# PSUM banks handed out by the planner, f16 hidden states, a float32r output projection and a product moved to GpSimd, in a one-core kernel of a gated recurrence and an FFT convolution

## The chip, the cores and the metric

One Trainium2 chip, one of its cores. The metric is the device time of one execution in microseconds (us). The engines are called as the profile calls them: PE (TensorE, its weight loads apart as PEld), DVE (VectorE), ACT (ScalarE), POOL (GpSimd) and SP (SyncE, which here only issues DMAs).

## The reference

Inputs are `x` and `f_logit`, 4 x 6272 x 256 in float32, a `lower_bound` per channel, a projection of 256 x 768, a filter of 6272 x 256 and an output projection of 256 x 256.

```python
sig = 1.0 / (1.0 + np.exp(-f_logit))
f = lower_bound + (1.0 - lower_bound) * sig
i = 1.0 - f
for t in range(S):                       # S = 6272
    h = f[:, t] * h + i[:, t] * x[:, t]
    y[:, t] = h
proj = y @ w_proj
x1, x2, x3 = proj[..., :D], proj[..., D:2*D], proj[..., 2*D:]     # D = 256
x2_conv = irfft(rfft(x2, axis=1) * rfft(filter, axis=0), axis=1)  # length 6272
out = (x1 * x2_conv * x3) @ w_out
```

## The kernel before

Everything runs on one core, batch after batch. The length 6272 is split as 49 x 128. Per batch there are these phases, each a function:

- `hgrn(b)`: 13 chunks of 512 time steps (the last has 128). `f_logit` and `x` are loaded (L238), ACT makes the sigmoid (L241), POOL multiplies (L243), PE transposes both into channel-major form in PSUM banks 6 and 7 (L252), ACT makes the forget gate `fTs` (L262), and DVE runs the recurrence as a scan (L266) into `hs`, float32r, two buffers. POOL copies `hs` as f16 into the long tile `HA` (L269). PE multiplies `hs` by the weights `W13`, float32r, for x1 and x3 (L277, banks 4 and 5); ACT copies x1 to `x1s` (L285) and DVE multiplies x3 by it into `z`, f16 (L288). Each chunk has two halves of 128 channels, `kh` on the way in and `jb` on the way out.
- `wraps()`: DMAs that copy pieces of `HA` into its middle part (L296), so that `phase_p` reads a cyclic sequence.
- `phase_p(b)`: x2, in 13 groups of four rows (L550), copied by ACT or DVE into `X2`.
- `phase_f1(b)`: first DFT step, 16 units (L565), copied into the middle part of `HA`, called `A`.
- `mini(b)`: the columns of frequency zero, which end in `zm`.
- `units(b)`: 16 units. Second DFT step on PE (L616), product with the transformed filter `Hu` on DVE (L626, two per unit), the zero columns from `zm` on POOL (L619), inverse step on PE (L637), copied to `Th` (which lies on `X2`). `Hu` has two buffers; each unit loads it from the DRAM tile `H[u]` by three DMAs (L609).
- `phase_o(b)`: 13 groups of four rows. Last inverse step on PE (L663), product with `z` on DVE into `PP` as f16 (L672), output projection on PE with the weights split into a high and a low f16 part, `Woh` and `Wol` (L685, four matmuls of 256 columns per row), copied to `osb` (L211) and stored (L696).

`prepare` runs once: the weights, the DFT tables, and the filter's transform, which starts with a rotation by a float32 matmul (L479), goes on with two float32r DFT steps (L496, L512) and stores `H[u]` to DRAM, one DMA per unit.

The order of the instructions is written out by a planner at build time. Each step is given to `op` with a cost per engine, the tiles it reads and the tiles it writes. `emit` is a list scheduler: of the steps whose predecessors have been placed it takes the one that can start earliest by its costs, the longest remaining path breaking ties. The order is then fixed in every engine's queue; the chip waits on semaphores. PSUM's banks are named in the steps, so two steps that use the same bank come in their order of declaration. `hgrn(b+1)` is planned together with `units(b)` and `phase_o(b)`, which keep to banks 0 to 3 except in the last batch. `prepare` and `hgrn(0)` are one call of `emit`; `wraps()` of batch 0 and all that follows are the second.

Of the kernel before, what the change touches and what calls it, by code (L numbers as in the profile page):

```python
# [9 lines left out]
F32 = mybir.dt.float32  # L10
# [11 lines left out]
S = 6272  # L22
# [28 lines left out]
class Plan:  # L51
# [5 lines left out]

    LAT = {"PE": 0.2, "ACT": 0.16, "DVE": 0.14, "POOL": 0.16, "SP": 0.0}
    OWN = {"PE": 0.0, "ACT": 0.1, "DVE": 0.08, "POOL": 0.1, "SP": 0.0}

    def __init__(self):
        self.ops, self.writer, self.readers = [], {}, {}
        self.free = {e: 0.0 for e in self.LAT}
        self.dma = 0.0
        self.table = None

    def op(self, cost, fn, r=(), w=(), kb=0.0, table=None):
# [8 lines left out]
        me = len(self.ops)  # L76
        self.ops.append(dict(cost=cost, fn=fn, preds=preds, kb=kb, table=table, end=None,
                             eng=None, succ=[]))
# [16 lines left out]

    def emit(self):
# [8 lines left out]
        while cand:  # L105
            best = None
            for e, f in self.free.items():
                pick = None
                for i in cand:
                    o = ops[i]  # L110
                    if e in o["cost"]:
                        at = max(f, self.ready(o, e))
                        if o["table"] and self.table and o["table"] != self.table:
                            at += 1.3
                        key = (at, -o["level"], i)
                        if pick is None or key < pick:
                            pick = key
                if pick is not None:
                    o = ops[pick[2]]
                    key = (pick[0] + (o["cost"][e] if len(o["cost"]) > 1 else 0.0) * 0.01,  # L120
                           pick[1], pick[2], e, pick[0])
                    if best is None or key < best:
                        best = key
            i, e, at = best[2:]
# [8 lines left out]
            o["fn"](e)  # L133
# [8 lines left out]
def kernel(  # L142
# [59 lines left out]

    def bank(*k):
        return [("b", i) for i in k]
# [23 lines left out]
    def hgrn(b):  # L228
        z = zt[b % 2]
        for c in range(NCHK):  # L230
# [14 lines left out]
            hk = c % 2  # L245
            for kh in range(2):
                cols = slice(kh * 128, kh * 128 + 128)
                sT, uT = PS[:, 6, 0:n], PS[:, 7, 0:n]

                def turn(e, dst, src, cols=cols, nb=nb):  # L250
                    for j in range(nb):
                        nc.tensor.transpose(dst[:, j * 128:(j + 1) * 128], src[:, j, cols],  # L252
                                            iden[:])
                op({"PE": 0.108 * nb}, lambda e, f=turn, d=sT, s=ft: f(e, d, s),
                   r=[("ft", k)], w=bank(6))
                op({"PE": 0.108 * nb}, lambda e, f=turn, d=uT, s=xt: f(e, d, s),
                   r=[("xt", k)], w=bank(7))
                j = count["f"] % 2
                count["f"] += 1
                fT, h = fTs[:, j, 0:n], hs[:, kh, hk, 0:n]  # L260
                op({"ACT": 0.13 + n / 1200.0}, lambda e, fT=fT, sT=sT, kh=kh:
                   nc.scalar.activation(fT, sT, AF.Identity, scale=nomc[:, kh:kh + 1],  # L262
                                        bias=1.0), r=bank(6), w=[("fT", j)])
                init = 0.0 if c == 0 else hs[:, kh, 1 - hk, CH - 1:CH].bitcast(F32)
                op({"DVE": 0.07 + 2.25 * n / 1000.0}, lambda e, h=h, fT=fT, uT=uT, init=init:
                   nc.vector.tensor_tensor_scan(h, fT, uT, init, op0=AOP.mult, op1=AOP.add),  # L266
                   r=bank(7) + [("fT", j), ("h", kh, 1 - hk)], w=[("h", kh, hk)])
                hn = HA[:, HB[kh] + t0:HB[kh] + t0 + n]
                op({"POOL": 0.1 + n / 1000.0}, lambda e, hn=hn, h=h: nc.gpsimd.tensor_copy(  # L269
                    hn, h.bitcast(F32)), r=[("h", kh, hk)], w=[("hn", kh, c)])  # L270
            for jb in range(2):
                for i in range(2):
                    js = slice(i * 256 + jb * 128, i * 256 + jb * 128 + 128)

                    def mm(e, i=i, js=js, hk=hk, n=n):
                        for kh in range(2):
                            nc.tensor.matmul(PS[:, 4 + i, 0:n], W13[:, kh, js],  # L277
                                             hs[:, kh, hk, 0:n], start=(kh == 0),
                                             stop=(kh == 1))
                    op({"PE": 2 * (0.06 + n / 2400.0)}, mm, r=[("h", 0, hk), ("h", 1, hk)],  # L280
                       w=bank(4 + i))
                j = count["s"] % 2
                count["s"] += 1
                xs = x1s[:, j, 0:n]
                op({"ACT": 0.06 + n / 1200.0}, lambda e, xs=xs, n=n: nc.scalar.activation(  # L285
                    xs, PS[:, 4, 0:n], AF.Copy, scale=ZS), r=bank(4), w=[("x1s", j)])
                op({"DVE": 0.07 + n / 960.0}, lambda e, zz=z[:, jb, t0:t0 + n], xs=xs, n=n:
                   nc.vector.tensor_tensor(zz, PS[:, 5, 0:n], xs, op=AOP.mult),  # L288
                   r=bank(5) + [("x1s", j)], w=[("z", b % 2, jb, c)])
# [12 lines left out]
    def prepare(tmp):  # L302
        dve, pool, act = nc.vector, nc.gpsimd, nc.scalar
        raws = [HA[:, S + 4096 * k:S + 4096 * (k + 1)].bitcast(F32)
                .rearrange("m (r d) -> m r d", d=D) for k in range(3)]
        hws = [HA[:, S + 12288 + 2048 * k:S + 12288 + 2048 * k + 1024]
               .rearrange("p (a n) -> p a n", a=2) for k in range(2)]
# [10 lines left out]
        def oms(e):  # L318
# [6 lines left out]
        wp = raws[0][:, 0:6].rearrange("p a d -> p (a d)").rearrange("p (k j) -> p k j", k=2)  # L325
        wo = raws[1][:, 0:2]
        op({"SP": 0.5}, lambda e: nc.sync.dma_start(
            wp, moe_w_proj.rearrange("(a p) j -> p a j", p=128)), w=E(0, 4096), kb=768)
        op({"SP": 0.5}, lambda e: nc.sync.dma_start(
            wo, moe_w_out.rearrange("(a p) j -> p a j", p=128)), w=E(4096, 8192), kb=256)  # L330
        for kh in range(2):
            small(lambda e, kh=kh: dve.tensor_scalar(
                wp[:, kh, :], in0=wp[:, kh, :], scalar1=omc[:, kh:kh + 1], scalar2=None,
                op0=AOP.mult), 768, r=["om"], w=E(0, 4096))
            for i, j0 in enumerate((0, 512)):
                small(lambda e, kh=kh, i=i, j0=j0: dve.tensor_copy(
                    W13[:, kh, i * 256:(i + 1) * 256], wp[:, kh, j0:j0 + 256]), 256,
                    r=E(0, 4096), w=["W13"])
            for p in range(2):
# [3 lines left out]
                    .rearrange("k (e g) -> k e g", e=2)), 256, r=E(0, 4096), w=["W2"])  # L343
        small(lambda e: dve.tensor_copy(Woh[:], wo[:]), 512, r=E(4096, 8192), w=["Wo"])
        small(lambda e: dve.tensor_tensor(Wol[:], wo[:], Woh[:], op=AOP.subtract), 512,
              r=E(4096, 8192), w=["Wo"])
# [105 lines left out]
        rot = tmp.tile([128, 256], F32, name="rot")  # L452
# [10 lines left out]
        small(gaps, 1920, r=["iden"], w=["f2e"], e="POOL")  # L463
# [297 lines left out]
```

## Time and profile before

| what | value |
|---|---|
| median of 3 runs | 731.81 us (728.07 to 734.73) |
| the profiled execution | 733.49 us |
| its span, first to last instruction | 731.7 us |
| mean granted TensorE clock in the span | 0.899 |
| busy: PE, DVE, ACT, POOL | 617.1, 513.9, 379.6, 203.2 us |
| DMA, mean over the span | 173 GB/s |

The span is what the profiled instructions cover; 1.8 us of the execution's own time lie outside it. A busy time counts an engine as busy from the start of an instruction to its modelled end, so PE's counts matmuls that overlap in its pipeline. "Releaser" is what ended an idle time.

### The profile page before, as it was taken

The numbers are of one execution on the slowest core, as the hardware profiler recorded it, in microseconds if no ns is written. First come the engines' busy times: TensorE is split into PE (matmuls) and PEld (weight loads), VectorE is DVE, ScalarE is ACT, GpSimd is POOL, SyncE is SP. The second block draws the span as 40 slices with busy tenths as digits, with TensorE's granted clock in tenths as the row PEclk, the third lists the DMA queues.
The fourth block names the chain that finished last, engine by engine and source line by source line (L and its number), as shares of the span: only waits on it lengthen the run. The fifth ranks groups of instructions, "written<-read, shape, count | busy, mean of one in ns | idle before, by whom it ended". The sixth has DMA issues, their size and how long they took to land. (4 is left out here: it accounts for less than half of the span.)

```text
span 731.7 us, 13373 instructions
## 1 busy us (share of the span) xinstructions
PE 617.1 (84%) x5262; PEld 471.1 (64%) x5262; DVE 513.9 (70%) x572; ACT 379.6 (52%) x485; POOL 203.2 (28%) x256
## 2 busy tenths in 40 slices
PE   4889993588878999888888999978769999677896
PEld 3767772574546887864556887845448888444585
DVE  8987772389787666697877665898676666967542
ACT  4578882485433555774333556854424547422232
POOL 4335451223323332033223333033324310010000
PEclk9999997699887999999778999999978999955599
DMA  9755646336565757155465766155746732034144
GB/s 308 279 167 162 204 151 232 127 88 204 182 194 175 241 194 268 41 175 175 160 201 181 239 216 239 58 168 181 215 149 227 242 151 82 22 115 131 45 193 160
DMA packets 82161, 126.95 MB, mean 173 GB/s; under 512 B 5454, under 2 KB 56722, under 8 KB 81330
## 3 DMA queue, kind: packets, MB, share of 16 engines
q1 hardware_dynamic: 82098, 126.10, 52.8%
q8 instruction: 41, 0.67, 0.4%
q14 instruction: 22, 0.18, 0.1%
HBM read 84.54 MB, written 28.90 MB: 155 GB/s over the span
## 5 line engine op out<-in xcount | busy, mean ns | idle before, releaser
L626 DVE TENSOR_TENSOR PP<-PS,Hu 98x1008 f16<-98x1008 f32 x128 | 147.8, 1198 | 46.1 <-DMA Hu<-H 37.0
L277 PE MATMUL PS<-hs,W 128*128 128x512 f32 (+1 forms) x416 | 140.5, 432 | 16.3 <-ACT x1s L285 10.9
L243 POOL TENSOR_TENSOR XT<-XT,FL 128x1024 f32<-128x1024 f32 (+1 forms) x52 | 116.7, 2244 | 86.0 <-DMA XT<-in_x_dram 61.2
L209 ACT CAST X<-PS 128x784 f16<-128x784 f32 (+2 forms) x86 | 87.1, 1020 | 86.4 <-PE PS L637 71.7
L269 POOL CAST HA<-hs 128x512 f16<-128x512 f32 (+1 forms) x104 | 61.6, 593 | 245.3 <-DVE hs L266 236.1
L266 DVE TENSOR_TENSOR_SCAN hs<-fTs,hs,PS 128x512 fp32r<-128x512 f32 (+1 forms) x96 | 115.9, 1207 | 10.6 <-PE PS L252 8.9
L672 DVE TENSOR_TENSOR PP<-PS,z 128x1024 f16<-128x1024 f32 (+1 forms) x52 | 61.1, 1184 | 82.7 <-PE PS L663 76.8
L262 ACT ACTIVATE fTs<-PS,nomc 128x512 f32<-128x512 f32 (+1 forms) x104 | 69.1, 665 | 80.1 <-DVE hs L266 42.6
L637 PEld LDWEIGHTS <-PP 98*128 98x128 f16 x1024 | 64.3, 118 | 51.0 <-issue 34.2
L685 PE MATMUL PS<-Woh,PP 128*128 128x256 f16 x392 | 90.3, 278 | 3.4 <-DVE PP L672 3.0
L685 PEld LDWEIGHTS <-PP 128*128 128x128 f16 x784 | 82.6, 114 | 15.8 <-issue 7.6
L277 PEld LDWEIGHTS PS<-hs,W 128*128 128x128 f32 x416 | 66.8, 196 | 35.3 <-ACT x1s L285 15.4
L685 PE MATMUL PS<-Wol,PP 128*128 128x256 f16 x392 | 89.0, 275 | 0.0
L616 PE MATMUL PS<-HA,FT 64*128 64x512 f16 x256 | 59.5, 458 | 31.7 <-DVE PP L626 30.3
L637 PE MATMUL PS<-VA,PP 98*128 98x98 f16 x512 | 72.9, 244 | 15.2 <-DVE PP L626 11.7
L211 ACT ACTIVATE osb<-PS 128x1024 f32<-128x1024 f32 (+1 forms) x51 | 50.3, 986 | 66.3 <-PE PS L685 37.5
L241 ACT ACTIVATE FL<-FL 128x1024 f32<-128x1024 f32 (+1 forms) x52 | 52.4, 1008 | 61.5 <-DMA FL<-in_f_logit_dram 61.5
L288 DVE TENSOR_TENSOR z<-PS,x1s 128x512 f16<-128x512 f32 (+1 forms) x104 | 67.1, 645 | 15.6 <-PE PS L277 9.9
L252 PE MATMUL PS<-iden,FL 128*128 128x128 f32 x392 | 67.1, 295 | 12.8 <-ACT FL L241 10.8
L285 ACT ACTIVATE x1s<-PS 128x512 f32<-128x512 f32 (+1 forms) x104 | 59.3, 570 | 28.9 <-DVE z L288 15.8
L637 PE MATMUL PS<-VB,PP 98*128 98x98 f16 x512 | 73.5, 245 | 0.0
L252 PE MATMUL PS<-iden,XT 128*128 128x128 f32 x392 | 69.9, 304 | 3.4 <-DVE hs L266 3.4
(89 smaller groups left out, 711.3 us busy)
## 6 DMA issues: line engine op xcount, KB each, us to landing
FL<-in_f_logit_dram SPq DMA_DIRECT2D x48, 512.0 KB
XT<-in_x_dram SPq DMA_DIRECT2D x48, 512.0 KB
out_dram<-osb SPq DMA_DIRECT2D x48, 512.0 KB
Hu<-H SPq DMA_DIRECT2D x64, 196.0 KB
Hu<-H SPq DMA_DIRECT2D x128, 98.0 KB
HA<-in_moe_filter_fft_dram SPq DMA_DIRECT2D x6, 1024.0 KB
HA<-HA SPq DMA_DIRECT2D x16, 384.0 KB
H<-HA SPq DMA_DIRECT2D x16, 196.0 KB
```

What stands on the lines that cost most here:

```text
L209: nc.scalar.copy(dst, src)
L243: op({"POOL": 0.1 + 0.535 * nb}, lambda e, xt=xt, ft=ft: nc.gpsimd.tensor_tensor(xt, xt, ft, op=AOP.mult), r=[("ft", k)], w=[("xt", k)])
L252: nc.tensor.transpose(dst[:, j * 128:(j + 1) * 128], src[:, j, cols], iden[:])
L262: nc.scalar.activation(fT, sT, AF.Identity, scale=nomc[:, kh:kh + 1], bias=1.0), r=bank(6), w=[("fT", j)])
L266: nc.vector.tensor_tensor_scan(h, fT, uT, init, op0=AOP.mult, op1=AOP.add),
L269: op({"POOL": 0.1 + n / 1000.0}, lambda e, hn=hn, h=h: nc.gpsimd.tensor_copy(hn, h.bitcast(F32)), r=[("h", kh, hk)], w=[("hn", kh, c)])
L277: nc.tensor.matmul(PS[:, 4 + i, 0:n], W13[:, kh, js], hs[:, kh, hk, 0:n], start=(kh == 0), stop=(kh == 1))
L288: nc.vector.tensor_tensor(zz, PS[:, 5, 0:n], xs, op=AOP.mult),
L626: nc.vector.tensor_tensor(PP[:TB, k, o, :, :, 1:64], px.unsqueeze(1).broadcast_to([TB, 2, UE, 63]), hh[:, :, :, 1:64], op=AOP.mult)
L637: nc.tensor.matmul(PS[:, ib + o, pr * TB:(pr + 1) * TB], PP[:TB, k, o, n, 2 * pr:2 * pr + 2, :], v[:TB], start=(n == 0), stop=(n == 1))
L672: nc.vector.tensor_tensor(y, PS[:, cb:cb + 2, 0:rn * 128].rearrange("p a (m i) -> p a m i", i=rn), zr[:, :, :, r0:r0 + rn], op=AOP.mult),
L685: nc.tensor.matmul(po[:, i, :], y[:, kh, :, i], w[:, kh, :], start=(n == 0), stop=(n == 3))
```

## The change

- **Planner.** PSUM has no fixed banks any more. A step that produces in PSUM takes one or two banks (`take`), the steps that read it name it as their source (`src`), and the banks come free when the last of them has been placed. `room` picks the free banks that are free earliest by plan; `held` keeps a step from taking banks while another predecessor of its readers is not placed. Among steps that can start within 0.6 us (`SLACK`) of the earliest, an engine takes the one with the longest remaining path.
- **Hidden states.** The scan writes f16 straight into `HA` and takes its start from the f16 column before; `hs` and POOL's copy (L269) go. `W13` is f16, so x1 and x3 are f16 matmuls.
- **x1*x3.** For one of the two halves (`jb` = 0) ACT copies x3 too, into a single buffer `x3s`, and POOL multiplies; for the other half DVE multiplies as before.
- **Output projection.** `Woh` and `Wol` become one float32r `Wo`; DVE writes the product into a float32r tile `ys` of its own with two buffers, and each row has two matmuls.
- **Filter.** `H[u]` in DRAM holds both arrangements (three DMAs store it, in `prepare`), one DMA per unit loads it, into three buffers. In `prepare` the raw filter comes in 13 loads into six buffers, each is copied to float32r by ACT, DVE or POOL, and the rotation is a float32r matmul.
- **Order.** `wraps()` of batch 0 is planned with `prepare` and `hgrn(0)`. In the middle part of `HA` (16384 columns) the transformed filter waits for its store at columns 6144 to 10240 (before: 12288 to 16384); `wraps` writes columns 0 to 6096 and 10240 to 16384.
- **Memory.** The second buffer of `osb` lies on the end of `X2`, so `phase_p(b+1)` waits for the stores from it, and POOL clears the gaps there again before each `phase_f1`.

The diff, cut (the planner's bookkeeping, the renaming of bank arguments in `phase_p`, `phase_f1`, `mini` and the copies are left out):

```diff
+    SLACK = 0.6
...
+    def room(self, n):
+        best = None
+        for b in range(0, 8, n):
+            if None not in self.bank[b:b + n]:
+                key = (max(self.bank[b:b + n]), n == 1 and self.bank[b ^ 1] is not None, b)
+                if best is None or key < best:
+                    best = key
+        return best
+
+    def held(self, i):
+        return any(self.ops[p]["end"] is None and p != i
+                   for j in self.ops[i]["users"] for p in self.ops[j]["preds"])
...
+                    if o["take"]:
+                        if rooms[o["take"]] is None or self.held(i):
+                            continue
+                        at = max(at, rooms[o["take"]][0])
...
+                    first = min(can)[0] + self.SLACK
+                    pick = min((c for c in can if c[0] <= first), key=lambda c: c[1:])
...
-    W13 = konst.tile([128, 2, 512], F32R, name="W13")
+    W13 = konst.tile([128, 2, 512], F16, name="W13")
-    Woh = konst.tile([128, 2, 256], F16, name="Woh")
-    Wol = konst.tile([128, 2, 256], F16, name="Wol")
+    Wo = konst.tile([128, 2, 256], F32R, name="Wo")
-    hs = konst.tile([128, 2, 2, CH], F32R, name="hs")
+    x3s = konst.tile([128, CH], F32, name="x3s")
-    H = [dram.tile([TB, 2, UE * 64], F16, name=f"H{u}") for u in range(NU)]
+    H = [dram.tile([TB, 2, 2, UE * 64], F16, name=f"H{u}") for u in range(NU)]
...
-                init = 0.0 if c == 0 else hs[:, kh, 1 - hk, CH - 1:CH].bitcast(F32)
+                init = 0.0 if c == 0 else HA[:, t1 - 1:t1]
...
-                op({"POOL": 0.1 + n / 1000.0}, lambda e, hn=hn, h=h: nc.gpsimd.tensor_copy(
-                    hn, h.bitcast(F32)), r=[("h", kh, hk)], w=[("hn", kh, c)])
...
+                if jb:
+                    op({"DVE": 0.07 + n / 960.0}, lambda e, p, zz=zz, xs=xs, n=n:
+                       nc.vector.tensor_tensor(zz, PS[:, p, 0:n], xs, op=AOP.mult),
+                       r=[("x1s", j)], w=[("z", b % 2, jb, c)], src=x13[1])
+                else:
+                    x3 = x3s[:, 0:n]
+                    op({"ACT": 0.06 + n / 1200.0}, lambda e, p, x3=x3, n=n:
+                       nc.scalar.copy(x3, PS[:, p, 0:n]), w=["x3s"], src=x13[1])
+                    op({"POOL": 0.1 + 2.15 * n / 1000}, lambda e, zz=zz, xs=xs, x3=x3:
+                       nc.gpsimd.tensor_tensor(zz, x3, xs, op=AOP.mult),
+                       r=[("x1s", j), "x3s"], w=[("z", b % 2, jb, c)])
...
-        rot = tmp.tile([128, 256], F32, name="rot")
+        rot = tmp.tile([128, 256], F32R, name="rot")
...
+            op({"POOL": 0.1 + 0.3 * rn, "ACT": 0.1 + 0.22 * rn, "DVE": 0.1 + 0.27 * rn},
+               lambda e, raw=raw, fr=fr, rn=rn: copy(e, fr[:, 0:rn], raw[:, 0:rn]),
+               r=et, w=[("af", g % 2)])
...
+            for i, (p0, p1, q0) in enumerate(((0, TB, 0), (0, Q, Q), (Q, TB, 0))):
+                op({"SP": 0.5}, lambda e, hw=hw, u=u, p0=p0, p1=p1, q0=q0, ab=min(i, 1):
+                   nc.sync.dma_start(H[u][p0:p1, ab], hw[q0:q0 + p1 - p0]),
+                   r=ht, w=[("H", u, i)], kb=2 * (p1 - p0))
...
+            h = (b * NU + u) % 3
+            op({"SP": 0.5}, lambda e, h=h, u=u: nc.sync.dma_start(Hu[:TB, h], H[u][:]),
+               r=[("H", u, i) for i in range(3)], w=[("Hu", h)], kb=400)
...
-                    for kh in range(2):
-                        for w in (Woh, Wol):
-                            nc.tensor.matmul(po[:, i, :], y[:, kh, :, i], w[:, kh, :],
-                                             start=(n == 0), stop=(n == 3))
-                            n += 1
-            op({"PE": 0.44 * rn}, proj, ...)
+                    for kh in range(2):
+                        nc.tensor.matmul(po[:, i, :], y[:, kh, :, i], Wo[:, kh, :],
+                                         start=(kh == 0), stop=(kh == 1))
+            po = op({"PE": 0.34 * rn}, proj, r=[("y", yk)], take=2)
...
             hgrn(0)
+            wraps()
             plan.emit()
...
+        ys = cv.tile([128, 2, 2, 512], F32R, name="ys")
+        osb = [cv.tile([128, 4, 256], F32, name="osb0"),
+               X2[:, NEP * TB:NEP * TB + 2048].bitcast(F32).rearrange("p (r e) -> p r e", e=256)]
```

More of the change, by code (lines that the diff above doesn't have):

```diff
@@ L123, in emit @@
                         best = key
+            assert best is not None
             i, e, at = best[2:]
@@ L132, in emit @@
                 o["end"] = self.dma + 1.0
-            o["fn"](e)
+            if o["take"]:
+                o["at"] = b = rooms[o["take"]][2]
+                self.bank[b:b + o["take"]] = [None] * o["take"]
+                o["fn"](e, b)
+            elif o["src"] is not None:
+                q = ops[o["src"]]
+                o["fn"](e, q["at"])
+                q["uses"] = q.get("uses", 0) + 1
+                q["done"] = max(q.get("done", 0.0), o["end"] + self.LAT[e])
+                if q["uses"] == len(q["users"]):
+                    self.bank[q["at"]:q["at"] + q["take"]] = [q["done"]] * q["take"]
+            else:
+                o["fn"](e)
             cand.remove(i)
@@ L282, in hgrn @@
+                    x13.append(op({"PE": 2 * n / 2400.0}, mm,
+                                  r=[("hn", 0, c), ("hn", 1, c), "W13"], w=["qX"], take=1))
                 j = count["s"] % 2
                 count["s"] += 1
[L284 to L289, printed above, removed]
+                xs, zz = x1s[:, j, 0:n], z[:, jb, t0:t0 + n]
@@ L594, in prod @@
                                     op=AOP.add)
-        op({"DVE": 2.0}, prod, r=bank(2, 3) + ["Hm", ("Hm", 0), ("Hm", 1)],
-           w=[("osb", k), "zm"])
+        op({"DVE": 2.0}, prod, r=["Hm", ("Hm", 0), ("Hm", 1)], w=[("osb", 0), "zm"], src=mm)
     def units(b):
@@ L629, in prod, with inv @@
                         op=AOP.mult)
-                op({"DVE": 1.15}, prod, r=bank(xb + o) + [("Hu", k, i) for i in range(3)],
-                   w=[("P", k, o)])
-            def inv(e, k=k, ib=ib):
+                op({"DVE": 1.2}, prod, r=[("Hu", h)], w=[("P", k, o)], src=f2)
+            def inv(e, ib, k=k):
                 for o in range(2):
```

267 lines of the change are left out of this document (128 added, 139 removed).

## The prediction

> **What bounds the kernel now.** I read the page's head first, then cut the span into its phases, then asked who waits in each.
>
> ```profile
> span 731.7 us, 13373 instructions
> PE 617.1 (84%) x5262; PEld 471.1 (64%) x5262; DVE 513.9 (70%) x572; ACT 379.6 (52%) x485; POOL 203.2 (28%) x256
> ```
>
> No engine fills the span, so the bound must change with the phase. The view of busy time by windows, with edges at the phases' first and last instructions (columns: window, length, busy time and instructions of PE, PEld, DVE, ACT and POOL, granted clock, DMA share, GB/s):
>
> ```profile
> 0.00:117.00 117.00, 99.90 (x595) 77.07 (x596) 91.53 (x163) 83.73 (x118) 52.78 (x74) 1.00 0.63 205
> 117.00:135.50 18.50, 0.81 (x4) 0.29 (x3) 0.29 (x1) 2.19 (x3) 4.65 (x4) 0.57 0.92 315
> 160.00:233.00 73.00, 58.06 (x473) 36.61 (x470) 61.42 (x61) 33.25 (x47) 24.98 (x33) 0.88 0.59 184
> 233.00:292.50 59.50, 59.09 (x532) 48.30 (x531) 37.74 (x41) 31.22 (x43) 20.32 (x20) 0.98 0.69 231
> 292.50:320.00 27.50, 24.02 (x258) 22.07 (x257) 19.50 (x16) 21.93 (x22) 4.27 (x4) 0.94 0.21 71
> 320.00:394.00 74.00, 61.02 (x464) 39.30 (x464) 60.24 (x60) 31.09 (x44) 23.67 (x33) 0.81 0.58 181
> 394.00:452.00 58.00, 57.60 (x522) 47.18 (x518) 36.59 (x40) 30.74 (x42) 20.01 (x20) 0.98 0.70 234
> 480.00:551.00 71.00, 54.20 (x444) 35.13 (x443) 56.86 (x57) 29.77 (x42) 21.98 (x31) 0.87 0.60 180
> 551.00:607.00 56.00, 55.86 (x508) 45.58 (x507) 36.56 (x38) 28.12 (x39) 17.36 (x18) 0.98 0.60 206
> 635.00:687.00 52.00, 37.92 (x316) 21.56 (x312) 37.64 (x35) 12.61 (x16) 5.05 (x16) 0.57 0.36 109
> 687.00:731.70 44.70, 36.73 (x392) 32.72 (x392) 15.37 (x14) 12.67 (x13) 0.00 (x0) 0.92 0.37 145
> ```
>
> In order: `prepare` with `hgrn(0)`; a hole; then, three times, `units(b)` with the first half of `hgrn(b+1)` (73, 74 and 71 us; I call it U) and `phase_o(b)` with the second half (59.5, 58 and 56 us; O), each followed by the 27.5 us of `phase_p` and `phase_f1`; last, U and O of batch 3 without a neighbour. O is PE's: busy 59.09 of 59.50, DVE 37.74. U is DVE's as far as it is anyone's: 61.42 of 73, and the rest of DVE's time is waiting. In the hole nothing computes. Who ended those waits (views of the waits: whole span, then 635:688):
>
> ```profile
> DVE PP L626 <- DMA Hu<-H: 37.0, 26, 3.3
> PE PS L550 <- DMA HA<-HA: 17.7, 2, 13.6
> POOL XT L243 <- DMA XT<-in_x_dram: 61.2, 29, 13.2
> DVE PP L626 <- DMA Hu<-H: 9.9, 10, 2.5
> ```
>
> (Total us, number, longest.) The hole is PE waiting for the wraps. DVE's largest wait in U is the filter load: 37.0 us in all, 9.9 of them in the last U, so about 9 in each of the others.
>
> **The change part by part.** Durations, by group of one form, and how closely matmuls follow each other (timeline: start, length; the last three are pieces of the chain that ended last):
>
> ```profile
> L626 DVE TENSOR_TENSOR PP<-PS,Hu 98x1008 f16<-98x1008 f32 x128 | 147.8, 1198 | 46.1 <-DMA Hu<-H 37.0 <-PE PS L616 7.0 <-PE PS L637 2.0
> L277 PE MATMUL PS<-hs,W 128*128 128x512 f32 x384 | 134.4, 443 | 14.6 <-ACT x1s L285 10.9 <-ACT HA L209 2.8 <-DVE z L288 0.9
> L685 PE MATMUL PS<-Woh,PP 128*128 128x256 f16 x392 | 90.3, 278 | 3.4 <-DVE PP L672 3.0
> L685 PEld LDWEIGHTS <-PP 128*128 128x128 f16 x784 | 82.6, 114 | 15.8 <-issue 7.6 <-DVE PP L672 7.2
> L277 PEld LDWEIGHTS PS<-hs,W 128*128 128x128 f32 x416 | 66.8, 196 | 35.3 <-ACT x1s L285 15.4 <-issue 6.6 <-DVE z L288 4.5
> L288 DVE TENSOR_TENSOR z<-PS,x1s 128x512 f16<-128x512 f32 x96 | 64.8, 675 | 11.4 <-PE PS L277 6.4 <-ACT x1s L285 4.9
> L269 POOL CAST HA<-hs 128x512 f16<-128x512 f32 x96 | 59.3, 618 | 226.3 <-DVE hs L266 217.0 <-PE PS L565 9.2
> L285 ACT ACTIVATE x1s<-PS 128x512 f32<-128x512 f32 x96 | 57.1, 595 | 25.4 <-DVE z L288 15.8 <-PE PS L277 4.7 <-DVE PP L672 3.4
> L243 POOL TENSOR_TENSOR XT<-XT,FL 128x1024 f32<-128x1024 f32 x48 | 113.8, 2371 | 84.4 <-DMA XT<-in_x_dram 60.3 <-PE PS L252 12.3 <-ACT x1s L285 3.7
> L479 PE MATMUL PS<-HA,rot 128*128 128x256 f32 x98 | 23.1, 383 | 0.0
> L496 PE MATMUL PS<-D1r,f 128*128 128x128 f32 x128 | 17.1, 277 | 0.0
> 25.88 3.62 PE L479 MATMUL PS<-HA,rot 128*128 128x256 f32 x16
> 105.09 1.09 PE L496 MATMUL PS<-D1r,f 128*128 128x128 f32 x8
> 111.27 1.21 PE L277 MATMUL PS<-hs,W 128*128 128x512 f32 x4
> 293.79 12.21 PE L550 MATMUL PS<-W,HA 128*128 128x256 f16 x95 [0.75 <-issue]
> 288.69 0.47 SPq L296 DMA_DIRECT2D HA<-HA  x1
> 700.84 3.68 PE PS L685 x32
> 704.53 1.00 PE PS L663 x16
> 705.55 1.24 DVE PP L672
> ```
>
> *Projection (PE, in O).* A dense run gives the pace of a matmul: its length less one duration, over the count less one. For f16 of 256 columns (3.68 - 0.278)/31 = 0.110 us, so today's 784 take 86 us, 21.6 per batch. Afterwards 392, f32r, each with a weight load of its own. No row shows f32r at 256 columns. Lower bound: the load hides, 0.110. Upper: it doesn't; L496, f32r of 128 columns, runs at (1.09 - 0.277)/7 = 0.116, so a load costs up to about 0.11 and a matmul 0.22. L277 lies between: (1.21 - 0.443)/3 = 0.256 for 512 columns, where f16 takes twice 0.110 = 0.22. I take the middle, 0.165: 98 x 0.165 = 16.2 per batch, **-5.4** in each O (bounds -10.8 and 0).
>
> [...]
>
> *x1 and x3 in f16.* 0.256 becomes 0.22: 104 per batch x 0.036 = **-3.7** (bounds: 0 where something else ends the matmul, -9 if every second one now waits for a whole load); the two windows of L288 alone (DVE busy and count) show how `hgrn(1)` is shared out:
>
> ```profile
> 160.00:233.00 73.00, 6.79 (x10) 0.88 0.59 184
> 233.00:292.50 59.50, 9.64 (x15) 0.98 0.69 231
> ```
>
> 15 of 26 halves run in O, so -2 there, the rest in U, where PE doesn't bind.
>
> O in all: -7.5. DVE, at 37.74 of 59.5, is not late next, so this is kept; I count **-8** with the freer banks, bounds -3 and -13. Three times: -24.
>
> *Products moved (DVE).* 13 per batch of 0.675 go, 8.8 us; 5 of the 10 in U, 3.4 us. ACT gets 13 copies of about 0.595 (L285), 7.7 us beside its 31 to 33 busy of 73. POOL loses the copy of 0.618 twice per chunk, 15.4 us per batch, and gains one product; L243 at half size is 1.19 us, so 15.4 again: POOL stays where it is. The copy's going also shortens the way from the last scan to the wrap by about 1 us.
>
> *Hu.* With two buffers a load may start when DVE leaves unit u-2 and must land within one unit's 2 x 1.198 = 2.4 us. With three it has 4.8, and SP issues one DMA for three. Longest wait now 3.3, so nearly all of it goes: -2/3 of 9 in each U (PE is late next: 58 us busy of 73, though it overlaps itself there), -8.5 of 9.9 in the last. Bytes stay the same. U: -3.4 - 6 = **-9**, bounds -3 and -14; three times -27. Last U: 16 x 2.4 = 38.4 plus 4 to fill and drain = 43, **-9**.
>
> *Last O.* The chain repeats 3.68 + 1.00 + 1.24 and a little, 6.0 us for two groups. 16 x 0.165 = 2.64 for 3.68: -1 each, 6.5 times: **-6** (bounds -2 and -11).
>
> *Wraps.* In the hole PE resumes 18.5 us after the last scan's stage; in batch 1 the wrap issued at 288.69 lets L550 go on at 293.79, 5.1 us later. So **-13** (bounds -8, if `prepare`'s stores crowd the queue: with 48 DMAs instead of 16 on SP beside the wraps, and -15).
>
> *Prepare.* L479: 98 at (3.62 - 0.383)/15 = 0.216 are 21 us; 49 at 0.165 are 8: PE -13, with f16 x1/x3 -17. Against it 13 copies to f32r, about 1.1 us each by two of L269 or L285, on three engines, and ACT's 7.7 for x3 while ACT has 83.73 of 117 busy. PE is at 99.90; half is kept: **-8** (bounds 0 and -18).
>
> *Costs.* `phase_p(b+1)` may not write `X2` before the last store from `osb`'s second buffer has landed; by the wrap's 5.1 us from issue to use and PE's lead of four groups, +2 or so each, less the 1 us of the copy: **+2** in all (bounds 0 and +12). The gap clearing on POOL hides under the 12.21 us of `phase_p`. DVE's f32r product and the scan's f16 end read PSUM as before: 0.
>
> Sum: -8 - 13 - 27 - 24 - 9 - 6 + 2 = -85. The profiled execution was 733.5, 1.7 over the median; 731.8 - 85 = 647, and I say **648**.
>
> **Rivals.**
> 1. *f32r loads don't hide* (0.22): +5.4 per O and +5 at the end, +21: 669. For: L496. Against: L277, longer than its load.
> 2. *PE goes cold in U.* Granted clock is 0.81 to 0.88 there and 0.57 in the last U, where PE has only the units' work. Less PE work could pull U towards 0.57. PE's 58 busy at 0.88 would be 58 x 0.88/0.57 = 90 at worst, against the 64 I expect; since a slower PE is also a busier one, I price it half way, +13 in each of three U's: 687. [...]
> 3. *The planner's banks miss the chip's timing.* Banks are promised by planned times; where DMA is late, PE stands at the head of its queue for a bank whose reader waits, with everything behind it. Then only engine work goes: U -3, O -5, the rest half (-17): 648 + 85 - 41 = 692.
> 4. *Slower: x3s.* One buffer. ACT's next x3 copy waits for POOL's product, which stands in POOL's queue behind L243, which waits for the load of x (61.2 us in 29 waits, 2.1 mean). ACT then holds everything behind it. At 2.1 us a chunk, 52 x 2.1 = 109: 648 + 109 = 757. It decides once L243's wait, 2.37 and 1.19 together pass a chunk's 9 to 10 us (117/13, 132/13); the mean of 5.7 doesn't, the longest wait of 13.2 does.
> 5. *No net change*: 3 and part of 4 together, 731.
>
> **How the numbers follow.** Forecast (620 to 665) 0.52; rival 1, 0.13; rival 2, 0.10; rival 3, 0.10; better than 620, 0.04; rival 4, 0.06; rival 5, 0.05. The bounds' sum is -119 at best, so 613; to 705 the first four cases are in, and 0.15 is left out. The measurement can't tell less than about 1%, 724 to 739. Faster 0.89, same 0.05, slower 0.06.
>
> **What would show it.** Projection: 392 matmuls, their pace 0.165 in a dense run. Hole: under 6 us between the last scan and `phase_p(0)`. U near 63 us with hardly a wait of DVE for Hu; last U 43 with 2.4 per unit; O near 51, PE still full. Wrong if ACT waits for POOL (rival 4), if waits for PE's banks lead in U (3), or if the clock in U is under 0.75 (2).

## The result, and the profile after

| | before | after |
|---|---|---|
| median | 729.94 us (725.30 to 734.73, 4 runs) | 707.48 us (703.32 to 709.47, 4 runs) |
| profiled execution, its span | 733.49, 731.7 us | 703.32, 701.4 us |

The ratio is 0.9684, 95% interval 0.9604 to 0.9765: 3.2% faster, where 11% were forecast. Of the 85 us, 30 came between the two profiled executions and 22 between the medians. Of four executions below, two of e3_slack0_hilo_dve (660.67 and 662.33 us, for 648.66 and 649.09) and one of e5_no_x (712.24, for 695.67 to 702.49) were slower than the rest, and the time given is the median of the others. First the head of the page of after:

```profile
span 701.4 us, 12441 instructions
PE 584.2 (83%) x4821; PEld 443.0 (63%) x4821; DVE 484.3 (69%) x518; ACT 409.4 (58%) x548; POOL 208.9 (30%) x211
```

The work did shrink: PE lost 33 us, DVE 30, and ACT gained 30. Then the busy time by windows of after (same columns as before). The first five are cut at the first matmul of each `phase_p`; the others are U and O of batch 0, U and O of batch 1, and U and O of the last batch:

```profile
0.00:139.80 139.80, 100.95 (x546) 69.48 (x546) 82.57 (x152) 94.15 (x136) 53.60 (x61) 0.86 0.61 204
139.80:289.50 149.70, 127.22 (x1110) 99.22 (x1109) 105.54 (x94) 87.33 (x111) 45.41 (x40) 0.91 0.69 225
289.50:441.60 152.10, 130.68 (x1129) 100.63 (x1128) 109.95 (x102) 86.40 (x117) 46.27 (x43) 0.91 0.56 184
441.60:588.40 146.80, 130.01 (x1140) 99.59 (x1140) 110.91 (x102) 87.18 (x119) 47.99 (x43) 0.93 0.58 191
588.40:701.40 113.00, 95.30 (x901) 74.05 (x899) 75.37 (x70) 54.28 (x68) 15.64 (x25) 0.92 0.29 104
...
165.30:208.40 43.10, 31.55 (x324) 19.50 (x324) 38.49 (x37) 17.54 (x21) 11.84 (x19) 0.76 0.54 163
208.40:289.50 81.10, 73.60 (x550) 60.39 (x551) 50.12 (x47) 49.50 (x72) 31.72 (x19) 0.98 0.80 269
314.50:365.00 50.50, 36.52 (x344) 21.91 (x342) 40.36 (x39) 19.10 (x27) 12.95 (x21) 0.77 0.50 152
365.00:431.50 66.50, 63.39 (x502) 53.79 (x501) 44.54 (x41) 38.17 (x55) 25.17 (x14) 0.99 0.76 259
611.50:653.50 42.00, 35.13 (x345) 19.54 (x345) 40.36 (x41) 18.23 (x28) 10.07 (x20) 0.88 0.39 126
653.50:701.40 47.90, 38.77 (x320) 35.45 (x317) 17.23 (x17) 15.01 (x19) 1.72 (x2) 0.92 0.34 135
```

Two things stand out. The first part is not 21 us shorter, it is 4 us longer than the 135.5 of before. And U and O are no longer what they were: U of batch 0 has shrunk to 43.1 us and O has grown to 81.1, because nearly all of `hgrn(b+1)` has moved from beside the units to behind them. DVE's scans alone (L305: busy time and count, clock, DMA share, GB/s), in U and in O of batch 0:

```profile
165.30:208.40 43.10, 0.08 (x1) 0.76 0.54 163
208.40:289.50 81.10, 31.11 (x26) 0.98 0.80 269
```

Put against the forecast, with the times from one `phase_p` to the next (P(0) to P(3) are their first matmuls; only for P(0) of before it is the first matmul after the hole, since three come ahead of the hole or in it, at 116.94 and 121.49; the last column is an experiment told below):

| part | before | after | change | forecast | after, with SLACK = 0 |
|---|---|---|---|---|---|
| start to P(0) | 135.5 | 139.8 | +4.3 | -21 | 119.7 (-15.8) |
| P(0) to P(3) | 474.9 | 448.6 | -26.3 | -49 | 432.6 (-42.3) |
| P(3) to the end | 121.3 | 113.0 | -8.3 | -15 | 110.8 (-10.5) |
| span | 731.7 | 701.4 | -30.3 | -85 | 663.1 (-68.6) |

The groups of one form of after, the waits that answer to those of before, and pieces of the timeline and of the chain that ended last:

```profile
L719 PE MATMUL PS<-Wo,ys 128*128 128x256 f32 x392 | 102.3, 406 | 6.8 <-DVE ys L709 6.8
L719 PEld LDWEIGHTS PS<-Wo,ys 128*128 128x128 f32 x392 | 94.1, 325 | 11.4 <-issue 6.8 <-DVE ys L709 3.3 <-ACT osb L249 0.8
L316 PE MATMUL PS<-HA,W 128*128 128x512 f16 x384 | 104.1, 397 | 2.9 <-DVE HA L305 1.4 <-ACT x1s L324 0.9 <-ACT x3s L333 0.6
L528 PE MATMUL PS<-afs,rot 128*128 128x256 f32 x49 | 11.1, 355 | 8.7 <-ACT afs L247 3.3 <-DVE f L252 2.1 <-ACT f L247 1.8
DVE PP L667 <- DMA Hu<-H: 4.8, 3, 2.0
ACT x1s L324 <- POOL z L335: 5.4, 9, 0.9
58.49 2.32 PE L316 MATMUL PS<-HA,W 128*128 128x512 f16 x10
661.32 3.94 PE PS L719 x16
```

The wait for `Hu` has gone from 37.0 to 4.8 us. ACT waits 5.4 us in all for POOL's product. The projection (L719) is the surprise of this view: 16 matmuls, two groups of rows, take 3.94 us in the chain, where 32 took 3.68.

### The profile page after: what moved, and what is told of

It reads as the page before. It is cut to its first block, busy times and chain, and to the rows that moved or that the text cites. A ratio compares the mean times of both kernels' runs of the same rounds, so it can differ in the third digit from the quotient of the medians.

```text
span 701.4 us, 12441 instructions
## 1 busy us (share of the span) xinstructions
PE 584.2 (83%) x4821; PEld 443.0 (63%) x4821; DVE 484.3 (69%) x518; ACT 409.4 (58%) x548; POOL 208.9 (30%) x211
## 5 line engine op out<-in xcount | busy, mean ns | idle before, releaser
L305 DVE TENSOR_TENSOR_SCAN HA<-fTs,HA,PS 128x512 f16<-128x512 f32 (+1 forms) x96 | 115.4, 1209 | 62.6 <-PE PS L288 55.3
L247 ACT CAST X<-PS 128x784 f16<-128x784 f32 (+2 forms) x91 | 90.7, 1010 | 89.7 <-PE PS L677 81.3
L316 PE MATMUL PS<-HA,W 128*128 128x512 f16 (+1 forms) x416 | 106.5, 384 | 4.1 <-DVE HA L305 1.4
L719 PE MATMUL PS<-Wo,ys 128*128 128x256 f32 x392 | 102.3, 406 | 6.8 <-DVE ys L709 6.8
L719 PEld LDWEIGHTS PS<-Wo,ys 128*128 128x128 f32 x392 | 94.1, 325 | 11.4 <-issue 6.8
L335 POOL TENSOR_TENSOR z<-x3s,x1s 128x512 f16<-128x512 f32 (+1 forms) x52 | 63.1, 1213 | 123.1 <-ACT x3s L333 123.0
L709 DVE TENSOR_TENSOR ys<-PS,z 128x1024 fp32r<-128x1024 f32 (+1 forms) x52 | 60.0, 1177 | 44.6 <-PE PS L702 36.7
L288 PEld LDWEIGHTS PS<-iden,XT 128*128 128x128 f32 x392 | 47.1, 147 | 34.3 <-POOL XT L281 21.4
L288 PEld LDWEIGHTS PS<-iden,FL 128*128 128x128 f32 x392 | 47.6, 148 | 28.5 <-ACT FL L279 19.2
L657 PE MATMUL PS<-HA,FT 64*128 64x512 f16 x256 | 47.5, 459 | 20.8 <-ACT X L247 20.1
L316 PEld LDWEIGHTS <-W 128*128 128x128 f16 x416 | 38.8, 101 | 39.0 <-issue 13.4
L702 PE MATMUL PS<-ID,X 64*128 64x128 f16 x784 | 50.9, 314 | 0.7 <-ACT fTs L300 0.3
```

The source lines that it names most:

```text
L247: nc.scalar.copy(dst, src)
L288: nc.tensor.transpose(PS[:, p, j * 128:(j + 1) * 128], src[:, j, cols], iden[:])
L305: nc.vector.tensor_tensor_scan(h, fT, PS[:, p, 0:n], init, op0=AOP.mult, op1=AOP.add),
L316: nc.tensor.matmul(PS[:, p, 0:n], W13[:, kh, js], HA[:, HB[kh] + t0:HB[kh] + t0 + n], start=(kh == 0), stop=(kh == 1))
L335: nc.gpsimd.tensor_tensor(zz, x3, xs, op=AOP.mult),
L709: nc.vector.tensor_tensor(y, PS[:, cb:cb + 2, 0:rn * 128].rearrange("p a (m i) -> p a m i", i=rn), zr[:, :, :, r0:r0 + rn], op=AOP.mult),
```

## The experiments

All are edits of the kernel after. Times are medians, ratios are against the kernel before on the same chip.

**The choice by longest path.** What moved the steps about? The planner's new rule takes, among the steps that can start within 0.6 us, the one with the longest remaining path; the other theory is that the banks do it.

```diff
-    SLACK = 0.6
+    SLACK = 0.0
```

> The changed kernel with SLACK 0.0 for 0.6: an engine takes the step that can start earliest again, banks still handed out by the planner. Theory A (the 0.6 us choice by longest remaining path puts hgrn(b+1) behind units(b), and the filter's DFT behind hgrn(0)): scans come back into U, U 43-52 -> about 60, O with its rest 80-82 -> about 55, phase_p(0) starts near 120 instead of 139.8; about 670 us. Theory B (the handing out of banks does it: the units' pairs of banks are taken ahead and hgrn's single banks find no room): order and time as the changed kernel, 700 to 710. Theory C (only the f32r projection's bare weight loads cost the forecast gain): no change either, 700 to 710.

663.48 us, ratio 0.9006 (0.8923 to 0.9089). With the banks named in the steps as in the kernel before, and 0.6 kept (`take=1` becomes `take=1, only=(6,)` for the first transpose, and so on):

> The changed kernel with each PSUM producer tied to the banks it had before (sT 6, uT 7, x1 4, x3 5, pairs as in the old code), SLACK 0.6 kept. Theory A: the choice still starves hgrn, 700 to 710. Theory B: two to three scans stand again between the units' products, U about 60, O about 55, 670 us; where only U and O are helped and not prepare, 685.

708.36 us, 0.9647 (0.9588 to 0.9705). P(0) comes at 136.1 us there, so the start is late without the free banks too. P(0) to P(3) takes 432.0 us, 16.6 less than in after, and P(3) to the end 137.4, against 113.0 with free banks.

With both undone, the old banks and SLACK = 0, about 665 us were expected. It took 711.24 us, 0.9705 (0.9631 to 0.9780), with P(0) at 133.2, 436.3 to P(3) and 140.9 to the end. (The output of this kernel is not the reference's, and why is open; only its times are used here.) So it takes both: SLACK = 0 gives its 44 us with free banks and nothing with the old ones, and the free banks give 48 us with SLACK = 0 and nothing with 0.6. Neither theory says that.

Where the 20 us of the first part went is seen in the two traces. Busy time by windows of the filter's first DFT step alone (L542: PE, PEld, clock, DMA share, GB/s), first after, then SLACK = 0:

```profile
0.00:50.00 50.00, 2.87 (x16) 2.73 (x16) 0.88 0.83 288
50.00:95.00 45.00, 0.21 (x1) 0.02 (x1) 0.94 0.60 197
95.00:139.80 44.80, 20.26 (x112) 18.17 (x112) 0.74 0.38 119
```

```profile
0.00:50.00 50.00, 2.12 (x16) 1.94 (x16) 0.90 0.82 291
50.00:95.00 45.00, 14.46 (x104) 12.76 (x104) 0.92 0.64 206
95.00:119.70 24.70, 1.11 (x8) 0.97 (x8) 1.00 0.71 249
```

And DVE's scans (L305) in the same windows, after and SLACK = 0:

```profile
50.00:95.00 45.00, 19.09 (x15) 0.94 0.60 197
95.00:139.80 44.80, 2.22 (x3) 0.74 0.38 119
```

```profile
50.00:95.00 45.00, 10.21 (x8) 0.92 0.64 206
95.00:119.70 24.70, 10.91 (x10) 1.00 0.71 249
```

With 0.6 the scans of `hgrn(0)` are taken first (the rule prefers the longer remaining path; that theirs is the longer is inferred), and 112 of 128 matmuls of the filter's DFT come when hardly a scan is left. That DFT is a chain from PE to ACT or DVE and back, so nothing lies beside it: in 95 to 139.8 PE runs at a clock of 0.74. With 0 the two lie beside each other. The wraps' hole has gone in both; in after the filter stands in its place.

**Which of the two plans.** SLACK = 0 in the first call of `emit` only (`prepare`, `hgrn(0)`, wraps), and its mirror, 0 in the second only:

```diff
+            plan.SLACK = 0.0    # e3_slack0_prepare: then 0.6 after emit
             plan.emit()
+            plan.SLACK = 0.0    # e4_late0: 0.6 before it
```

> SLACK 0.0 only while prepare, hgrn(0) and wraps(0) are planned, 0.6 for all that follows. Theory A by place: phase_p(0) starts near 120 as with SLACK 0.0 throughout, the later batches stay at 147 to 152 us from phase_p to phase_p: 707 - 20 = 687. If the whole 44 us hang on the first plan (the order of batch 0 carried on): 665. If on the later plan: 705.

> SLACK 0.6 in the first plan, 0.0 in the second: the mirror of the run with 0.0 in the first alone (666). Theory D (the first plan costs its 20 us by the 0.6 us choice; the rest of the difference in the batches is a draw among orders of about equal worth, in which the changed kernel had a bad one): phase_p(0) at 140, the three batches 416 to 437 together, as in all other variants, and not 449: 680 to 700. Theory A in full (the 0.6 us choice costs in the batches too, by rule): three batches near 425 here. Theory E (order carried on from the first plan): batches stay at 449, 705.

666.20 us, 0.913 (0.9083 to 0.9177), and 689.43 us, 0.9459 (0.9387 to 0.9532). So, with free banks, the first plan alone gives back nearly all of the 44 us that SLACK = 0 gives. (The mirror's 18 are hardly more than the draw between orders that is measured below. Its three batches took 441.2 us, which none of the three theories had.) The first matmul of `phase_p(0)`, timeline of after, of e1_slack0, of e3_slack0_prepare and of e4_late0:

```profile
139.78 1.07 PE L598 MATMUL PS<-W,HA 128*128 128x256 f16 x4
```

```profile
119.71 0.52 PE L598 MATMUL PS<-W,HA 128*128 128x256 f16 x3 [0.26 <-ACT x1s L324]
```

```profile
120.89 0.52 PE L598 MATMUL PS<-W,HA 128*128 128x256 f16 x3 [0.26 <-ACT x1s L324]
```

```profile
136.49 1.07 PE L598 MATMUL PS<-W,HA 128*128 128x256 f16 x4
```

Over all runs told of here with free banks and the wraps in the first plan, P(0) lies at 113.9 to 124.4 us with 0 there and at 139 to 145 with 0.6 (136.5 in e4_late0). The time from P(0) to P(1) tends to follow it: 138 to 145 us with 0, 142 to 156 with 0.6, though the costs and the rule of the second plan may be the same. Why is open. From after to e3_slack0_prepare it falls by 9 us, from 149.7 to 140.9; about 5 of them lie in U of batch 0 (43.1 us at a clock of 0.76 in after, 37.9 at 0.86 in e3_slack0_prepare).

Does it matter that the wraps moved into the first plan? SLACK = 0, and `wraps()` of batch 0 back in the second plan:

> SLACK 0.0 with wraps() of batch 0 planned after the first plan's end again, behind the clearing of X2. Forecast: the hole comes back, phase_p(0) 13 us later: 663 + 13 = 676. If the hole only went because the filter's DFT now runs to the end of the first plan: 663 to 666.

662.95 us, 0.9091 (0.9021 to 0.9161). The hole is back: three matmuls of `phase_p(0)` come at 128.8, and the long run behind the hole starts at 134.95, as in before (135.54), where with SLACK = 0 alone it starts at 121.11.

```profile
134.95 13.34 PE L598 MATMUL PS<-W,HA 128*128 128x256 f16 x95 [5.35 <-DMA HA<-HA]
```

So moving the wraps is worth 14 us where the hole lies, close to the forecast's 13. P(3) comes at 551.7 all the same, for 552.3: the batches behind the hole took 14 us less, and the total showed none of it. Neither reason in the expectation fits.

**The projection.** The two f16 parts back in place of float32r, the planner told 0.44 per row:

```diff
-    Wo = konst.tile([128, 2, 256], F32R, name="Wo")
+    Woh = konst.tile([128, 2, 256], F16, name="Woh")
+    Wol = konst.tile([128, 2, 256], F16, name="Wol")
...
-            po = op({"PE": 0.34 * rn}, proj, r=[("y", yk)], take=2)
+            po = op({"PE": 0.44 * rn}, proj, r=[("y", yk)], take=2)
```

> The changed kernel with the old projection: ys in f16, Woh and Wol, four f16 matmuls per row instead of two f32r. By the paces read from the two traces (392 x 0.234 = 92 us against 784 x 0.109 = 86) PE loses 6 us in all, all of it in O, which PE bounds. Theory C: the projection is what ate the gain, over 20 us faster, 685. Theories A and B: 6 us faster at most, 700.

686.46 us, 0.9352 (0.9298 to 0.9407). With SLACK = 0:

> SLACK 0.0 and the old f16 projection (Woh and Wol) together, everything else of the change kept. If the two losses are separate they add: 663 less the 20 that the old projection gave with SLACK 0.6 = 643. If the projection's 20 us came only from an O overfull with hgrn (SLACK's doing), it gives the 6 us of the paces here: 657.

652.17 us, 0.8905 (0.8821 to 0.8988). Better by 21 and by 11 us. But the planner's cost had changed too, so that was done alone, float32r kept and 0.34 set to 0.47, near what the chip takes (two matmuls of 0.236):

> The changed kernel with SLACK 0.6 and the f32r projection, but the planner is told 0.47 us per row for it (two matmuls at the measured 0.234) instead of 0.34. If the projection cost 20 us because the planner believed it cheap and put the steps behind it at the wrong times, 687 to 692. If it is the matmuls' own pace and their bare loads, 702 to 708.

> SLACK 0.0 and the honest 0.47 us per row for the f32r projection. Each alone gave 44 and 17. If the wrong cost does harm apart from SLACK: 663 - 12 = 651, level with the old projection under SLACK 0.0 (652). If it only misled the 0.6 us choice: 660 to 665.

690.90 us, 0.9456 (0.9390 to 0.9522), and 653.28 us, 0.8956 (0.8889 to 0.9023). Nothing that runs had changed but its order, and 17 and 10 us went. So the totals don't show that the f16 parts are faster.

Is it float32r that makes the matmul slow? The trace of after answers that. The rotation (L528) is float32r of 256 columns too, each matmul with a load of its own, and runs at nearly the f16 pace, 0.13 us for the 0.110 of before (first line; the clock was 1.00). Its loads are shorter than the projection's (next two lines: min/median/max in ns). They read 128 neighbouring elements of `rot`, while the projection's loads read every fourth element of `ys`, except in the last group of a batch, which has one row and so reads neighbours (last line):

```profile
31.88 1.22 PE L528 MATMUL PS<-afs,rot 128*128 128x256 f32 x8 [0.64 <-DVE f L252]
L528 PEld LDWEIGHTS PS<-afs,rot x49: 186/189/333, 15.6 to 46.2; 128*128 128x128 f32 x49
L719 PEld LDWEIGHTS PS<-Wo,ys x392: 186/329/334, 214.8 to 696.1; 128*128 128x128 f32 x196
L719 PEld LDWEIGHTS PS<-Wo,ys x2: 190/191/192, 267.8 to 268.0; 128*128 128x128 f32 x2
```

L528's pace is (1.22 - 0.282)/7 = 0.13 us, with 0.282 as the median duration of these eight. The last line is the same instruction at a step of one, 190 ns for 329, so here it is the step at which `ys` is read that makes the load long. (The f16 loads of before read `PP` at the same step and took 114 ns.) An estimate: 392 matmuls at 0.13 would be 51 us of PE for 92. A `ys` laid out for that was not run.

**Hu.** With SLACK = 0 and only two of the three buffers of `Hu` in use, 689 us were expected if the third buffer cures DVE's waits, 663 to 668 if not. It took 667.81 us, 0.9133 (0.9070 to 0.9196). DVE waits 26.6 us in all for `Hu` there, against 9.2 with three buffers and SLACK = 0. So the third buffer does what the forecast says of it, and the total hardly shows it. (This output is not the reference's either, and why is open.)

**Products.** Both halves multiplied by DVE, no copy of x3, SLACK = 0 (`if jb:` becomes `if True:`), and the same with the f16 parts:

> SLACK 0.0 and both halves of x1*x3 multiplied on DVE from PSUM as before, no copy of x3, nothing on POOL. Forecast's theory: DVE gets 8.8 us per batch back, 3.4 of them in U: 663 + 10 = 673. Rival (the copy on ACT and the queue of POOL cost more than they free): 650 to 660.

> SLACK 0.0, old f16 projection, both halves of x1*x3 on DVE: what is left is the handed-out banks, f16 h, H in three buffers, the f32r rotation and the early wraps. If the two losses add: 663 - 11 - 9 = 643. If both only loosened the same O: 650 to 655.

654.72 us, 0.8955 (0.8893 to 0.9016), and 648.88 us, 0.8896 (0.8829 to 0.8963). POOL's half is worth nothing that shows.

**How much is the order's own draw?** By now I no longer trusted a difference of 10 us to an edit. Costs that the planner alone sees were moved by a few per cent: the units' product 1.2 to 1.3, the inverse step of `phase_o` 0.235 to 0.25, the first also with SLACK = 0.

```diff
-            op({"DVE": 1.2}, ...
+            op({"DVE": 1.3}, ...
```

> The changed kernel, SLACK 0.6 throughout; only the planner's cost of the unit's product is 1.3 for 1.2. Nothing of the first plan moves, the order of the second does. Theory D: phase_p(0) stays at 140, the three batches fall from 449 to somewhere in 416 to 440 without any cause by rule: 685 to 705. Theory A in full: batches stay within 5 us of 449, 702 to 710.

> The same with the planner's cost of phase_o's inverse step at 0.25 per row for 0.235, the product back at 1.2. Theory D: phase_p(0) at 140, three batches somewhere in 416 to 449, another value than in the run before: 680 to 708. Theory A in full: 702 to 710.

> SLACK 0.0 throughout and 1.3 for 1.2. Shows how wide the draw is without the 0.6 us choice. Theory D: phase_p(0) at 120, three batches 416 to 440 where SLACK 0.0 alone had 433: 645 to 670. If the order is no draw but a rule: 661 to 666.

692.28 us, 0.9484 (0.9436 to 0.9533); 705.26, 0.9666 (0.9612 to 0.9720); 655.17, 0.8976 (0.8917 to 0.9035). Orders of the same work differ by 15 us, so an edit that makes the planner choose again can't be priced by the total below that. What differs is seen in U of batch 1 (windows; after is 314.50:365.00 above): first e4_prod13, then e3_slack0_prepare's U of batches 1 and 2:

```profile
318.80:359.30 40.50, 31.07 (x346) 18.00 (x345) 38.71 (x39) 17.92 (x27) 10.71 (x20) 1.00 0.54 162
```

```profile
285.60:337.80 52.20, 38.52 (x341) 23.01 (x341) 40.23 (x39) 18.90 (x27) 12.98 (x21) 0.71 0.50 146
439.80:479.10 39.30, 30.48 (x334) 17.78 (x335) 38.20 (x38) 17.22 (x25) 10.23 (x20) 0.96 0.56 168
```

The same 340 matmuls and 39 DVE instructions take 50 to 52 us where the granted clock is 0.71 to 0.77, and 39 to 41 where it is 0.96 to 1.00. Inside the U of after the clock dips, comes back for 10 us, and falls again at 345 to stay down (windows of 5 us):

```profile
325.00:330.00 5.00, 3.70 (x46) 2.44 (x44) 4.52 (x5) 1.88 (x3) 0.65 (x2) 1.00 0.66 188
330.00:335.00 5.00, 3.10 (x22) 1.57 (x21) 2.30 (x3) 2.85 (x4) 0.00 (x0) 0.66 0.95 246
335.00:340.00 5.00, 3.22 (x41) 1.97 (x41) 3.78 (x5) 2.12 (x4) 4.32 (x5) 1.00 0.38 111
340.00:345.00 5.00, 2.85 (x42) 1.88 (x43) 5.00 (x5) 1.92 (x3) 0.65 (x2) 1.00 0.57 167
345.00:350.00 5.00, 4.10 (x36) 2.52 (x36) 3.79 (x4) 0.81 (x1) 0.33 (x1) 0.52 0.58 193
350.00:355.00 5.00, 3.20 (x29) 2.06 (x28) 3.83 (x4) 1.62 (x2) 0.65 (x2) 0.50 0.36 118
```

At 0.50 DVE is busy 3.8 of 5 us; at 1.00 it was busy 3.8 to 5.0. What sets it off? In this U ACT stands once for a load of `f_logit`, with PE and DVE behind it (first line, in 314.50 to 365.00; the second line is PE's longest wait in total):

```profile
ACT FL L279 <- DMA FL<-in_f_logit_dram: 2.8, 1, 2.8
PE PS L657 <- ACT X L247: 11.3, 10, 3.2
```

and e4_prod13 has neither wait in its U. That gave a theory to test: the same order on every compute engine, with the loads of `f_logit`, and in the other kernel those of `x`, left out for batches 1 to 3.

```diff
+                left = b > 0 and t[0] == "ft"       # the other kernel: "xt"
-                op({"SP": 0.5}, lambda ...: nc.sync.dma_start(
+                op({"SP": 0.5}, lambda ...: None if left else nc.sync.dma_start(
```

> The order of every engine as in the changed kernel; only the loads of f_logit for batches 1 to 3 are left out (ACT works on what the tile holds), so the output isn't the reference's. In the changed kernel the units of batches 1 and 2 take 50.2 and 52.4 us at a granted clock of 0.77 and 0.80, and in each of them ACT waits once, 2.8 and 2.1 us, for a load of f_logit, with PE and DVE behind it; where a run had no such wait they took 40.5 and 41.7 at 1.00. Theory F (this one wait stops PE, the granted clock falls to 0.50 after it, and the rest of the units runs at that): without the load U of batches 1 and 2 takes 40 to 44 us at 0.9 or more, and the run 680 to 690. Theory G (the clock falls because PE has few matmuls in this order, or the order itself is long): U stays at 49 to 53 at under 0.82, and the run within 5 us of 703. Theory H (it is POOL's wait for x, 6.3 and 4.7 us, that stops the rest): no change here either, but in the other kernel of this call.

> The same with the loads of x left out for batches 1 to 3 in place of those of f_logit. Theory F: ACT still waits for f_logit once in the units of batches 1 and 2; U stays near 48 to 53 us with the clock under 0.85, unless the lighter queue brings f_logit early. Theory G: the same. Theory H: U falls to 40 to 44 us, and the run to 680 to 690.

699.36 us, 0.9578 (0.9503 to 0.9653), and 700.38 us, 0.9596 (0.9526 to 0.9665). Theory F falls, and H with it; in after itself the clock had come back to 1.00 for 10 us between that wait and the fall that stayed. U of batch 1 without the loads of `f_logit`, whole and in its middle, and PE's waits between 319 and 331 us, ahead of the fall:

```profile
308.80:359.20 50.40, 37.57 (x342) 22.64 (x342) 40.19 (x39) 18.85 (x27) 12.80 (x21) 0.71 0.47 141
334.00:339.00 5.00, 3.20 (x30) 2.12 (x29) 3.97 (x4) 1.62 (x2) 0.65 (x2) 0.50 0.47 152
PE PS L659 <- ACT X L247: 2.3, 3, 0.9
PE PS L679 <- DVE PP L669: 1.1, 2, 0.6
```

The wait for `f_logit` is gone, and the clock falls all the same, with no wait of PE longer than 0.9 us ahead of it. So theory G is what is left: it is in the order. Which feature of the order decides between a U at 0.7 and one at 1.0 was not tested. One feature goes with the length of U: L657, the second DFT step, waits for ACT's copy L247, which writes nothing that L657 reads, so it waits for the PSUM banks that this copy empties. That wait comes to 11.3 us in U of batch 1 of after, 11.4 in e3_slack0_prepare's U at 0.71 and 9.5 in e5_no_flogit's. It is missing from the three U's at 0.96 to 1.00 (e4_prod13's of batches 1 and 2, e3_slack0_prepare's of batch 2). In after it is there, 0.9 us each time, while the clock still is 1.00 (335 to 345). By itself it doesn't decide the clock: a U of e2_cost47 had 7.2 us of it at 1.00 and took 46.4 us.

## Why the prediction was wrong, and where it was right

- **The step that failed: the choice within 0.6 us was given no price.** The change lists it, and no term of the sum, and no rival, says what it reorders. *Prepare* (-8) and *Wraps* (-13) became +4.3. The wraps' hole did go, but the filter's DFT took its place; with SLACK = 0 in the first plan the two terms come to -14 to -16. The run with 0 in the first plan alone, e3_slack0_prepare, gives back 41 of the 44 us that SLACK = 0 gives: 19 ahead of P(0), 9 between P(0) and P(1), and 9 up to P(3). The last two lie within the draw, and the rest is the profiled execution against the median. This holds with free banks; with the old banks SLACK = 0 gave nothing (711.24 for 708.36).
- **U and O as the prediction cut them no longer exist.** It took for granted that half of `hgrn(b+1)` stays beside the units. U and O of batch 0 come to 124.2 us against 132.5 (-8, forecast -17). With SLACK = 0 the scans stay more evenly shared (57.8 and 55.9 us in batch 0) and the three batches reach -42 of -49. But with 0 in the first plan alone, U of batch 0 is as short as in after (37.9) and the three batches come to 430.9: where the scans stand decided little there. That PE was busy 73.41 of the 78.7 us behind the units may be why; this was not tested.
- **Projection: the size of a term.** Pace forecast 0.165 us, bounds 0.110 and 0.22; measured (3.94 - 0.406)/15 = 0.236, above the upper bound. Two of them take 0.47, the four f16 ones took 0.44. So -5.4 per O became about +1.6, and the last O, forecast -6, got slower in its chain by 0.3 per two groups. The bounds came from L277 and L496, whose loads read neighbouring elements and took 196 and 192 ns; the loads of `ys` read every fourth and took 325 on average. Rival 1 gave nearly the right price for another reason: L528's loads (189 ns) mostly hide, its matmuls follow each other at 0.13. 98 x (0.236 - 0.165) = 7.0 per batch, 28 us in four O's, is the largest mis-sized term, and about the 30 us missing behind P(0). But SLACK = 0 gets 18 of these 30 back with the projection as it is, so the sizes don't simply add. Where both read neighbours, a float32r load took 189 ns and an f16 one 98 (medians of L528 and L316), and L528's pace, 0.13 for the 0.110 of f16, shows that this alone costs little.
- **f16 x1 and x3: right.** Forecast 0.22; (2.32 - 0.397)/9 = 0.214.
- **Rotation:** L528 is 11.1 us of PE for 23.1, near the -13 forecast; it did not bind.
- **Hu: right.** 37.0 became 4.8, and the last U went from 52 to 42.0 (forecast 43). Its clock rose too, from 0.57 to 0.88; the two were not separated.
- **Rival 2 (the granted clock falls in U) happened in part.** Forecast +13 in each U if it came; the two middle U's of after, at 0.77 and 0.80, take some 10 us more each than those of e4_prod13 at 1.00. My mark for it, under 0.75 over the whole U, was set too low: half a U at 0.50 and half at 1.00 reads about 0.75.
- **Rival 4 (x3s) did not happen:** ACT waited 5.4 us in all for POOL.
- **Rival 3 (banks) happened in part:** its sign, waits for PE's banks leading in U, came true in the middle U's (11.3 us in batch 1). It explains neither the late start, which came with the old banks too, nor the total by itself: with the old banks the batches took 16.6 us less and the end 24 us more. Its time, 692, is near the result by luck.
- **A slip in the bounds:** their sum at best is -134 (598 us), not -119 (613); the -15 of *Wraps* was left out.

The 648 us of the forecast is about what the change gives once the choice is off: 663, and 652 to 655 with one more edit; these last four (e2_slack0_hilo, e3_slack0_cost47, e2_slack0_dve, e4_s0_prod13) can't be told apart, and each beats both kernels. That doesn't bear out the sum: the projection's -22 is in none of them, and orders alone differ by up to 15 us.

## What to carry to other kernels

When a change touches the scheduler, price what it reorders first: ask which long chain it puts ahead, and what is then left alone at the end with nothing beside it. Before believing a single edit's total under such a scheduler, nudge a cost that only the planner sees and look at the spread; read the edit itself by a local number (a pace, one wait, one phase). Before replacing two f16 matmuls by one in float32r, look at the load of its weights in the layout that will be read: read at a step of four elements it took 329 ns here, read as neighbours 189.

## What the runs showed of the hardware

- A float32r matmul of 256 columns with a load of its own follows the last at 0.236 us where the load reads every fourth element (L719, load 329 ns median), and at 0.13 where it reads neighbours (L528, 189 ns). Two f16 ones with loads took 2 x 0.110, at a step of four elements as well (L685 of before, load 114 ns).
- In U of batch 1 of after the granted clock was 1.00 from 335 to 345 us, with 41 and 42 matmuls per 5 us and PE busy 3.2 and 2.9 of them; then it fell to 0.50 and stayed there for the 20 us to the end of the units, with 29 to 36 matmuls per 5 us. The same work in another order held 1.00 throughout (U of batch 1 of e4_prod13, 43 to 50 matmuls in each 5 us behind the first).
- Within e4_s0_prod13 the mean granted clock goes with the time: its four runs had 649.1, 650.8, 655.6 and 656.8 us of span at 0.956, 0.946, 0.944 and 0.941. It isn't so in every kernel: e1_slack0 had 654.2 us at 0.939 and 660.3 at 0.946.
